# The second layer's first product by Strassen's seven products, with its steps put in order by a list scheduler

## The chip, the cores and the metric

The kernel runs on one core of one Trainium2 chip. The metric is the device time of one execution in microseconds (us), the median of several runs. Engines: PE (TensorE: matmuls; PEld, its weight loads), DVE (VectorE), ACT (ScalarE), POOL (GpSimd), SP (the queue that issues the DMAs).

## What is computed

Windowed attention over 4 batches of 576 tokens gives x, 2304 tokens of 512 values. Two feed-forward layers follow, each with weights `w_in` (512x2048) and `w_out` (2048x512), which arrive as float64:

```
layer 1:  h = x @ w_in;  Q = 1 + |b0|*|h| + |b1|*h*h;  P = a0 + a1*h + a2*h^2 + a3*h^3
          x = (P / (Q + 1e-6)) @ w_out
layer 2:  h = x @ w_in;  g = h if h > 0 else exp(h) - 1
          out = g @ w_out
```

## The kernel before

**Tiling.** The 2304 tokens are cut into 6 blocks of 384 (`TB`), the 2048 hidden values into 16 rows of 128 (`KF`). One row of one block is a chunk: 96 chunks per layer. x lies transposed in `xT` (4 slices of 128 x 2304), and layer 1 writes its result back into it.

**Precision.** Every operand of a product is split into a high and a low fp32r part, and a product runs as three passes (`PASS`: high*high, low*high, high*low). `gemm1` (line 243) makes one chunk of h with 4 slices x 3 passes = 12 matmuls of 128x384. Layer 1's second product (`gemm2_T`, line 696) takes 12 such matmuls per chunk, layer 2's (`gemm2`, line 734) 9 matmuls of 128x512.

**Weights.** A float64 weight tile is joined to float32 and then split: `conv_scale` (ACT), `conv_shift`, `conv_or`, `conv_sign` (three DVE operations on 128x512, lines 145, 152, 159), `conv_hi` (ACT) and `conv_lo` (POOL, line 173). `conv_step` works on three tiles at a time, one at each stage. Layer 1's 32 tiles are converted during attention, the last of them in block 0 of layer 1; layer 2's 32 tiles are loaded and converted from block 5 of layer 1 on, in the slots that layer 1's weights leave (`renew`).

**Order.** All instructions are issued in the order in which the program is written, and each engine works through its own queue in that order. The loop of `experts` (line 764) takes one chunk a turn: `gemm1` of chunk s, then the second product of chunk s-3 (`SK = 3`), then the elementwise work of chunk s. In layer 1 that is `rational` (line 264): on DVE the rest of chunk s-1 and the start of chunk s are interleaved, six operations, and the last one of a chunk, `glo` (line 307), is on POOL. In layer 2 it is `elu` and `elu_split`: two activations on ACT and three operations on DVE. `split_x` makes the fp32r parts of a new block of x.

Of the kernel before, what the change touches and what calls it, by code (L numbers as in the profile page):

```python
# [44 lines left out]
def kernel(  # L45
# [45 lines left out]
    order = [(w, f) for f in range(2 * KF) for w in ("wi", "wo")]  # L91
    order[2 * KF:] = sorted(order[2 * KF:], key=lambda key: 2 * key[1] + 3 * (key[0] == "wo"))
    SLOT = {key: key for key in order[:2 * KF]}


    LATE = order[2 * KF - 8:2 * KF]
    to_load, to_conv = order[:2 * KF], order[:2 * KF]


    ends = {(w, f): f + 3 * (w == "wo") for w, f in order[:2 * KF]}  # L100
    for_x = [("wi", f) for f in range(8)]
    slots = [key for key in sorted(ends, key=ends.get) if key not in for_x] + for_x
    SLOT.update(zip(order[2 * KF:], slots))

# [159 lines left out]
    def rational(c, old=True):  # L264
# [41 lines left out]
        if old:  # L306
            nc.gpsimd.tensor_tensor(out=lo, in0=ee0, in1=rr0, op=ALU.mult)  # L307


# [367 lines left out]
    def experts():  # L677
        es = ctx.enter_context(ExitStack())
        tmp.append(es.enter_context(tc.tile_pool(name="tmp", bufs=1)))
        psum = es.enter_context(tc.tile_pool(name="ps_moe", bufs=1, space=PSUM))  # L680


        def at_rows(c):
            tags = (("h2", "oo"), ("rr0", "rr1"), ("ee0", "ee1"), ("ghi3", "glo3"))[c]
            return [row(t, F32R) for t in tags]

        def at_pieces(j, c):
            t = place(for_x[4 * j + c], [P, 2, TB], F32R, "xs")
            return t[:, 0], t[:, 1]

        def renew(slot):
            key = next(key for key in order[2 * KF:] if SLOT[key] == slot)
            load_w(key)
            to_conv.append(key)
# [20 lines left out]
        def elu(c):  # L715
            h = h_t.pop(c)
            e = row(f"qq{c % 2}")
            nc.scalar.activation(out=e, in_=h, func=AF.Exp)  # L718
# [6 lines left out]
            return e

        def elu_split(c, e):
            hi = row(f"ghi{c % 3}", F32R)
            lo = row(f"glo{c % 3}", F32R)
            nc.scalar.activation(out=hi, in_=e, func=AF.Copy)  # L730
            nc.vector.tensor_tensor(out=lo, in0=e, in1=hi.bitcast(F32), op=ALU.subtract)  # L731
            g_t[c] = (hi, lo)

        def gemm2(c, j, f):
            gt = g_t.pop(c)
            conv_until(to_conv, ("wo", KF + f))
            if f == 0:
                for t in range(NTT):
                    acc_t[j, t] = bank((j % 2) * NTT + t, [P, DM], "acc")
            for t in range(NTT):  # L740
# [6 lines left out]
                if f == KF - 1:
                    o = cv.tile([P, DM], F32, tag="cvt", name="osb")
                    nc.scalar.activation(out=o, in_=acc_t[j, t], func=AF.Copy)
                    r0 = j * TB + t * P  # L750
                    nc.sync.dma_start(out=out[r0:r0 + P, :], in_=o)


        chunks = [(j, f) for f in range(KF) for j in range(2)]
        chunks += [(j, f) for j in range(2, NB) for f in range(KF)]

        SK = 3
        LAST = NCH - KF
        own = {}

        def split_part(parts, j, c, where):
            split_row(parts.setdefault(j, {"hi": [], "lo": []}), j, c, where, nc.vector)
# [87 lines left out]
```

## Time and profile before

| | us |
|---|---|
| median of 3 runs (lowest, highest) | 980.83 (979.93, 981.08) |
| the profiled execution | 979.8 |
| its span, first to last instruction | 978.1 |
| PE busy / DVE / ACT / POOL | 945.8 / 740.6 / 628.3 / 275.9 |

The profile is of one execution. Its busy time of PE counts matmuls whose ends are modelled and that overlap; how fast PE works is read from the distance between the starts of its matmuls. On DVE and ACT, too, the next instruction starts before the record of the one before ends, so what an instruction costs in a full queue is the distance from start to start.

### The profile page before, as it was taken

How to read it: one execution, taken by the hardware profiler on the slowest of the kernel's cores; microseconds unless marked ns; L12 is line 12 of the kernel's file. 1: busy time of each engine (PE TensorE's matmuls, PEld its weight loads, DVE VectorE, ACT ScalarE, POOL GpSimd, SP SyncE). 2: the span in 40 equal slices, each digit the busy share in tenths (PEclk: the TensorE clock that was granted, in tenths of full speed). 3: DMA queues.
4: the chain of work that ended last, by engine and by line, in shares of the span. 5: the costliest groups of instructions: out<-in, count | busy, mean ns of one | idle time of the engine just before them, and what ended most of it. 6: DMA issues, size and time to landing. Idle time of an engine off the chain costs nothing.

```text
span 978.1 us, 16050 instructions
## 1 busy us (share of the span) xinstructions
PE 945.8 (97%) x5638; PEld 865.2 (88%) x5638; DVE 740.6 (76%) x1553; ACT 628.3 (64%) x1368; POOL 275.9 (28%) x315
## 2 busy tenths in 40 slices
PE   7999998989999999999999998999999999999998
PEld 4767667989999999999999986999999999999997
DVE  5999989999998898889889999899543343343332
ACT  5999999779788788788888754555342332322322
POOL 5777764332322222223224342233100000000000
PEclk9999999999999999999999998999999999999999
DMA  6798751000000000000016712200010000000000
GB/s 169 208 248 235 207 160 51 1 1 1 1 1 1 1 1 1 1 1 1 1 44 201 224 50 87 87 1 1 6 60 1 33 1 1 33 1 1 34 1 32
DMA packets 82065, 53.47 MB, mean 55 GB/s; under 512 B 59200, under 2 KB 75584, under 8 KB 81984
## 3 DMA queue, kind: packets, MB, share of 16 engines
q1 hardware_dynamic: 81984, 52.45, 18.2%
q8 instruction: 44, 0.72, 0.3%
q14 instruction: 37, 0.30, 0.1%
HBM read 47.71 MB, written 4.72 MB: 54 GB/s over the span
## 4 chain that ended last, share of the span: by engine, by line
PE 73%; DVE 14%; ACT 9%; issue 3%; DMA 0%; POOL 0%; DVEq 0%; SPq 0%; POOLq 0%; ACTq 0%
PE h L249 35%; PE acc L742 19%; PE acc L705 17%; ACT pT L426 2%; DVE cvt L152 2%; ACT pr_wo L500 2%; ACT pr_wi L500 2%; DVE ghi L287 1%; DVE qq L289 1%; DVE qq L297 1%; DVE ee L305 1%; DVE raw_wo L145 1%; DVE oo L301 1%; ACT cvt L141 1%; DVE cvt L159 1%
## 5 line engine op out<-in xcount | busy, mean ns | idle before, releaser
L249 PE MATMUL h<-xs,w_wi 128*128 128x384 f32 x1260 | 237.4, 335 | 1.8 <-DVE xs L225 0.9
L249 PEld LDWEIGHTS h<-xs,w_wi 128*128 128x128 f32 x1260 | 219.8, 188 | 4.2 <-DVE xs L225 1.5
L705 PE MATMUL acc<-ghi,w_wo 128*128 128x384 f32 x768 | 194.9, 334 | 0.0
L307 POOL TENSOR_TENSOR glo<-ee,rr 128x384 fp32r<-128x384 f32 x96 | 115.7, 1206 | 280.3 <-DVE ee L303 234.6
L742 PE MATMUL acc<-w_wi,ghi 128*128 128x512 f32 x468 | 146.8, 395 | 0.0
L705 PEld LDWEIGHTS acc<-ghi,w_wo 128*128 128x128 f32 x768 | 138.6, 188 | 0.0
L705 PE MATMUL acc<-glo,w_wo 128*128 128x384 f32 x384 | 129.0, 336 | 7.4 <-POOL glo L307 7.4
L718 ACT ACTIVATE qq<-h 128x384 f32<-128x384 f32 x96 | 47.0, 490 | 137.9 <-PE h L249 137.9
L719 DVE TENSOR_SCALAR qq<-qq 128x384 f32<-128x384 f32 x96 | 37.7, 393 | 118.0 <-ACT qq L718 117.2
L730 ACT ACTIVATE ghi<-qq 128x384 fp32r<-128x384 f32 x96 | 50.3, 524 | 97.7 <-PE acc L742 79.8
L287 DVE TENSOR_TENSOR ghi<-ee,rr 128x384 fp32r<-128x384 f32 x96 | 98.5, 1026 | 9.8
L742 PEld LDWEIGHTS acc<-w_wi,ghi 128*128 128x128 f32 x468 | 87.6, 190 | 14.7
L731 DVE TENSOR_TENSOR glo<-qq,ghi 128x384 fp32r<-128x384 f32 x96 | 53.4, 556 | 56.2 <-ACT ghi L730 56.2
L742 PE MATMUL acc<-w_wi,glo 128*128 128x512 f32 x234 | 93.3, 399 | 0.0
L249 PE MATMUL h<-xs,w_wo 128*128 128x384 f32 x408 | 78.2, 338 | 4.6 <-DVE xs L225 3.6
L705 PEld LDWEIGHTS acc<-glo,w_wo 128*128 128x128 f32 x384 | 72.1, 188 | 9.4 <-POOL glo L307 9.3
L249 PEld LDWEIGHTS h<-xs,w_wo 128*128 128x128 f32 x408 | 72.5, 188 | 8.8 <-DVE xs L225 4.2
L289 DVE SCALAR_TENSOR_TENSOR qq<-h,b_abs,qq 128x384 f32<-128x384 f32 x96 | 63.3, 660 | 21.0 <-ACT qq L275 21.0
L293 ACT ACTIVATE rr<-qq,c_q 128x384 f32<-128x384 f32 x96 | 58.9, 614 | 25.5 <-DVE qq L289 24.7
L279 ACT ACTIVATE ee<-h,a_sb 128x384 f32<-128x384 f32 x96 | 67.7, 705 | 4.1 <-POOL glo L307 1.9
L276 ACT ACTIVATE oo<-h,a_sb 128x384 f32<-128x384 f32 x96 | 67.9, 707 | 0.0
L274 ACT ACTIVATE h<-h 128x384 f32<-128x384 f32 x96 | 46.4, 483 | 32.1 <-PE h L249 32.1
(146 smaller groups left out, 1789.8 us busy)
## 6 DMA issues: line engine op xcount, KB each, us to landing
raw_wi<-in_moe_w_in_dram SPq DMA_DIRECT2D x19, 512.0 KB, 4.3
raw_wo<-in_moe_w_out_dram SPq DMA_DIRECT2D x19, 512.0 KB, 4.8
raw_wo<-in_moe_w_in_dram SPq DMA_DIRECT2D x13, 512.0 KB, 4.6
raw_wi<-in_moe_w_out_dram SPq DMA_DIRECT2D x13, 512.0 KB, 4.6
out_dram<-osb SPq DMA_DIRECT2D x18, 256.0 KB, 2.0
v<-in_v_dram SPq DMA_DIRECT2D x32, 128.0 KB, 2.8
q_wi<-in_q_dram SPq DMA_DIRECT2D x16, 128.0 KB, 4.7
k_wi<-in_k_dram SPq DMA_DIRECT2D x16, 128.0 KB, 3.9
```

What stands on the lines that cost most here:

```text
L249: nc.tensor.matmul(h, lhsT=WT["wi", f][:, SEL[wp], kk * P:(kk + 1) * P], rhs=x[xp][kk], start=(kk == 0 and n == 0), stop=(kk == KD - 1 and ...
L276: nc.scalar.activation(out=oo, in_=h2, func=AF.Identity, scale=a_sb[:, 3:4], bias=a_sb[:, 1:2])
L279: nc.scalar.activation(out=ee, in_=h2, func=AF.Identity, scale=a_sb[:, 2:3], bias=a_sb[:, 0:1])
L287: nc.vector.tensor_tensor(out=hi, in0=ee0, in1=rr0, op=ALU.mult)
L289: nc.vector.scalar_tensor_tensor(out=qq, in0=h2, scalar=b_abs[:, 1:2], in1=qq, op0=ALU.mult, op1=ALU.add)
L293: nc.scalar.activation(out=rr, in_=qq, func=AF.Ln, bias=c_q)
L307: nc.gpsimd.tensor_tensor(out=lo, in0=ee0, in1=rr0, op=ALU.mult)
L705: nc.tensor.matmul(acc_t[d], lhsT=WT["wo", f][:, SEL[wp], d * P:(d + 1) * P], rhs=gt[SEL[xp]], start=(f == 0 and n == 0), stop=(f == KF - ...
L718: nc.scalar.activation(out=e, in_=h, func=AF.Exp)
L730: nc.scalar.activation(out=hi, in_=e, func=AF.Copy)
L731: nc.vector.tensor_tensor(out=lo, in0=e, in1=hi.bitcast(F32), op=ALU.subtract)
L742: nc.tensor.matmul(acc_t[j, t], lhsT=gt[SEL[xp]][:, t * P:(t + 1) * P], rhs=WT["wo", KF + f][:, SEL[wp], :], start=(f == 0 and n == 0), st ...
```

## The change

**Strassen.** Layer 2's `gemm1` goes. Two neighbouring weight rows (a pair, p = 0 to 7) and two neighbouring blocks (J = 0 to 2) make a step q = 8J + p, 24 in all, and the four chunks of a step come from seven products (`product`) of half the depth, 2 slices x 3 passes = 6 matmuls of 128x384 each: 42 where four calls of `gemm1` had 48. The operands are a11, a12, a22 and four sums s1 to s4 of quarters of the weights (`sum_w`, four POOL operations of 128x256 per step), and b11, b21, b22 and four differences t1 to t4 of quarters of x (`sum_x`, eight operations of 128x384 per J; on DVE for J = 0, on POOL for J = 1 and 2). The seven results are put together by one copy on ACT (`copy_of`) and seven additions on DVE (`added`, line 943). All of them pass through two PSUM banks in turn.

**The elementwise work of layer 2** is now exp, minus one (ACT), one DVE operation (`rest`, line 958), the high part (ACT) and the low part (DVE, `lo`, line 847). Per step DVE also makes the low parts of six weight operands (five 128x512, one 128x256), and per J those of 14 operands of x.

**Weights of layer 2.** Twenty of the 32 tiles (`early_ones`) are loaded in halves during blocks 0 to 4 of layer 1, joined there (`join_scale` on ACT, `join_words` with three DVE operations of 128x256) and stored as float32 in DRAM; `load_wi` and `load_wo` read them back in every J. 40 half tiles are joined, ten in each of blocks 1 to 4. The other twelve `w_out` tiles are joined in steps 0 to 7 (one tile in steps 0 to 3, two in 4 to 7) by `join_wo`, three DVE operations of 128x512.

**Layer 1.** `glo` moves from POOL to DVE. In block 5 `prepare` makes the operands of step 0 that can be made by then.

**Order of layer 2.** `second(q)` describes each piece of work as a step with an engine, a cost in ns and what it needs. `in_order` simulates the engines with these costs: PE's steps keep the order in which they are written, the other engines take, of the steps that are ready within 60 ns of the earliest, the one due first. The program is then issued in the order of the starts that it found.

```diff
@@ rational
+        if beside:
+            beside()
...
-            nc.gpsimd.tensor_tensor(out=lo, in0=ee0, in1=rr0, op=ALU.mult)
+            nc.vector.tensor_tensor(out=lo, in0=ee0, in1=rr0, op=ALU.mult)
@@ experts: layer 1's loop
-        for s in range(2 * NCH + SK):
+        for s in range(NCH):
...
+            if j > 0 and f % 3 and f < KF - 1 and nj < 2 * len(early_ones):
+                rational(s, beside=lambda: join_words(nj))
+                nj += 1
+            else:
+                rational(s)
+            if j > 0 and f % 3 < 2 and f < KF - 2:
+                join_scale(nj)
+                load_half(nj + 1)
...
+            if s >= LAST:
+                prepare(s - LAST)
+        rational(NCH)
+        for q in range(NQ):
+            second(q)
+        for fn in in_order():
+            fn()
+        last_pair()
@@ experts: layer 2
+        def product(q, nm):
+            x, side = LIES[FACTOR[nm]]
+            w = OPS[q, x]
+            out = bank((4 if q == 0 else 6) + next(ny), [P, TB], "m")
+            for k in range(2):
+                c0 = side * HC + k * P
+                for n, (wp, xp) in enumerate(PASS):
+                    nc.tensor.matmul(
+                        out, lhsT=w[:, SEL[wp], c0:c0 + P], rhs=XO[q // NP2, nm, k][:, SEL[xp]],
+                        start=(k == 0 and n == 0), stop=(k == 1 and n == 2),
+                    )
+            return out
...
+        def second(q):
+            p = q % NP2
+            multiply(q, "b11", (q - 1, "h21"))
+            multiply(q, "b21", (q - 1, "h12"))
+            second_product(q, 0)
+            multiply(q, "t2", (q, "m1"))
+            multiply(q, "t3", (q, "h11"))
+            second_product(q, 1)
+            multiply(q, "t1", (q, "u"))
+            second_product(q, 2)
+            multiply(q, "t4", (q, "v"))
+            multiply(q, "b22", (q, "h22"), (q, "u2"))
+            second_product(q, 3)
...
+        def prepare(f):
+            if f == 1:
+                load_wi(0)
+            if 3 <= f < 7:
+                sum_x(0, f - 3, nc.vector)
+            if f == 7:
+                sum_w(0, nc.vector)
+            if 8 <= f < 12:
+                hi_w(0, "ABCD"[f - 8])
+                lo((0, "ABCD"[f - 8]))
+            if 7 <= f < 11:
+                for k in range(2):
+                    hi_op(0, ORDER[f - 7], k)
+                for k in range(2):
+                    lo((0, ORDER[f - 7], k))
```

`second_product(q, n)` is the second product (9 matmuls of 128x512) of one chunk of step q-1; `last_pair` makes those of the last step.

**Where instructions move.** DVE in the middle of layer 1, one chunk. Before:

```order
L287 TENSOR_TENSOR ghi_5826<-ee_5776,rr_5785 128x384
L289 SCALAR_TENSOR_TENSOR qq_5819<-h_5818,b_abs,qq_5819 128x384
L297 SCALAR_TENSOR_TENSOR qq_5774<-qq_5774,ghi_5826 128x384
L301 TENSOR_TENSOR oo<-oo,h 128x384
L303 TENSOR_TENSOR ee_5776<-ee_5776,qq_5774 128x384
L305 TENSOR_TENSOR ee_5821<-ee_5821,oo 128x384
```

And now, a chunk that joins half a weight tile:

```order
L286 TENSOR_TENSOR ghi_4331<-ee_4278,rr_4287 128x384
L288 SCALAR_TENSOR_TENSOR qq_4324<-h_4323,b_abs,qq_4324 128x384
L764 TENSOR_SCALAR half_4199<-half_4199 128x256
L768 SCALAR_TENSOR_TENSOR whole_3175<-whole_3175,half_4199 128x256
L771 SCALAR_TENSOR_TENSOR whole_3175<-half_4199,whole_3175 128x256
L298 SCALAR_TENSOR_TENSOR qq_4276<-qq_4276,ghi_4331 128x384
L302 TENSOR_TENSOR oo<-oo,h 128x384
L304 TENSOR_TENSOR ee_4278<-ee_4278,qq_4276 128x384
L306 TENSOR_TENSOR ee_4326<-ee_4326,oo 128x384
L308 TENSOR_TENSOR glo_4332<-ee_4278,rr_4287 128x384
```

The low part (`glo`) has come from POOL to the end of the chunk's row, and three operations on half a weight tile stand ahead of the rest of the older chunk.

DVE in layer 2, from the first addition of a step with two raw `w_out` tiles (`qq`, `ee`: the sums of products `m`; `op`: weight operands; `pair`: the joined `w_out`):

```order
L943 TENSOR_TENSOR qq_8128<-qq_8107,m 128x384
L847 TENSOR_TENSOR rr_8113<-oo,rr_8112 128x384
L847 TENSOR_TENSOR op_wo_8124<-s_8069,op_wo_8124 128x512
L847 TENSOR_TENSOR op_wi_8126<-s_8070,op_wi_8126 128x512
L943 TENSOR_TENSOR ee_8155<-qq_8107,m 128x384
L958 SCALAR_TENSOR_TENSOR h_8142<-h_8142,qq_8128 128x384
L943 TENSOR_TENSOR ee_8167<-ee_8155,m 128x384
L138 TENSOR_SCALAR raw_wo_8089<-raw_wo_8089 128x512
L145 SCALAR_TENSOR_TENSOR pair<-pair,raw_wo_8089 128x512
L152 SCALAR_TENSOR_TENSOR pair<-raw_wo_8089,pair 128x512
L847 TENSOR_TENSOR glo_8170<-h_8142,ghi_8169 128x384
L847 TENSOR_TENSOR op_wi_8130<-pair,op_wi_8130 128x512
```

The additions that empty the PSUM banks (line 943) stand between the splits of weights and the joining of a tile for later steps.

PE in layer 2, from the start of a step; each x3 is half of a product, each x2 with the row behind it a third of a second product:

```order
L887 MATMUL m<-xo_wo_6762,op_wi_7546 128x384 x3
L887 MATMUL m<-xo_wi_6764,op_wi_7546 128x384 x3
L887 MATMUL m<-xo_wo_6816,op_wi_7546 128x384 x3
L887 MATMUL m<-xo_wi_6818,op_wi_7546 128x384 x3
L903 MATMUL acc<-op_wo_7601,ghi_7811 128x512 x2
L903 MATMUL acc<-op_wo_7601,glo_7812 128x512
L903 MATMUL acc<-op_wo_7601,ghi_7811 128x512 x2
L903 MATMUL acc<-op_wo_7601,glo_7812 128x512
L903 MATMUL acc<-op_wo_7601,ghi_7811 128x512 x2
L903 MATMUL acc<-op_wo_7601,glo_7812 128x512
L887 MATMUL m<-xo_wo_6870,op_wo_7672 128x384 x3
L887 MATMUL m<-xo_wi_6872,op_wo_7672 128x384 x3
```

Where one chunk's product of 12 matmuls and one second product took turns, two products of 6 matmuls now stand before most of the second products.

## Rows read from the trace of the kernel before

**Rows 1.** Busy time by stretch: us, PE, PEld, DVE, ACT, POOL, PEclk, DMA share, GB/s.
```profile
160.00:200.00 40.00, 36.85 (x210) 35.89 (x209) 39.01 (x61) 31.21 (x59) 14.31 (x12) 1.00 0.00 1
440.00:480.00 40.00, 40.00 (x232) 40.00 (x232) 36.48 (x62) 32.23 (x61) 11.74 (x10) 1.00 0.00 1
600.00:640.00 40.00, 35.47 (x162) 31.32 (x163) 35.58 (x59) 19.45 (x39) 10.43 (x8) 0.91 0.15 53
760.00:800.00 40.00, 40.00 (x202) 36.20 (x201) 15.71 (x33) 12.88 (x26) 0.00 (x0) 1.00 0.05 21
```

**Rows 2.** Chain that ended last: start us, length us, engine, tile, line, instructions.
```profile
607.91 3.84 PE acc L742 x9
611.75 2.67 PE h L249 x12
...
622.80 2.08 PE acc L742 x9
...
964.00 2.10 PE h L249 x12
966.10 8.22 PE acc L742 x36
```

**Rows 3.** Waits of PE over the whole span: us in total, times, longest.
```profile
PE acc L705 <- POOL glo L307: 7.4, 6, 1.5
...
PE h L249 <- DVE xs L225: 4.5, 3, 3.0
...
PE h L249 <- ACT xs L224: 1.6, 3, 0.7
```

**Rows 4.** Busy time by stretch around the longest wait.
```profile
602.00:606.00 4.00, 1.06 (x3) 0.48 (x3) 3.84 (x6) 2.12 (x4) 1.33 (x1) 1.00 0.00 0
606.00:610.00 4.00, 2.77 (x7) 2.31 (x8) 3.06 (x6) 1.99 (x4) 0.90 (x1) 0.50 0.01 2
```

**Rows 5.** DVE in order of time, one chunk of layer 1: start us, length us.
```profile
304.48 1.16 DVE L287 TENSOR_TENSOR ghi<-ee,rr 128x384 fp32r<-128x384 f32 x1
305.56 0.61 DVE L289 SCALAR_TENSOR_TENSOR qq<-h,b_abs,qq 128x384 f32<-128x384 f32 x1
306.09 0.55 DVE L297 SCALAR_TENSOR_TENSOR qq<-qq,ghi 128x384 f32<-128x384 f32 x1
306.56 0.54 DVE L301 TENSOR_TENSOR oo<-oo,h 128x384 f32<-128x384 f32 x1
307.02 0.55 DVE L303 TENSOR_TENSOR ee<-ee,qq 128x384 f32<-128x384 f32 x1
307.49 0.55 DVE L305 TENSOR_TENSOR ee<-ee,oo 128x384 f32<-128x384 f32 x1
308.17 1.16 DVE L287 TENSOR_TENSOR ghi<-ee,rr 128x384 fp32r<-128x384 f32 x1
```

**Rows 6.** POOL in order of time, the same chunk.
```profile
304.05 1.17 POOL L307 TENSOR_TENSOR glo<-ee,rr 128x384 fp32r<-128x384 f32 x1 [4.99 <-DVE ee L303]
```

**Rows 7.** DVE in order of time: one weight tile joined in layer 2.
```profile
641.04 1.27 DVE L145 TENSOR_SCALAR raw_wo<-raw_wo 128x512 int32<-128x512 int32 x1
642.41 0.69 DVE L152 SCALAR_TENSOR_TENSOR cvt<-cvt,raw_wo 128x512 int32<-128x512 int32 x1
643.14 0.69 DVE L159 SCALAR_TENSOR_TENSOR cvt<-raw_wo,cvt 128x512 int32<-128x512 int32 x1
643.75 0.55 DVE L731 TENSOR_TENSOR glo<-qq,ghi 128x384 fp32r<-128x384 f32 x1
```

**Rows 8.** POOL in order of time, beside it.
```profile
640.73 1.29 POOL L173 TENSOR_TENSOR w_wi<-cvt,w_wi 128x512 fp32r<-128x512 f32 x1 [2.88 <-ACT w_wi L169]
```

**Rows 9.** Line 145 during attention: duration in ns, least/median/most.
```profile
L145 DVE TENSOR_SCALAR raw_wo<-raw_wo x14: 406/420/427, 31.5 to 153.8; 128x512 int32<-128x512 int32 x14
```

**Rows 10.** DMA issues on the page: instructions, KB each, median us to landing.
```profile
raw_wo<-in_moe_w_out_dram SPq DMA_DIRECT2D x19, 512.0 KB, 4.8
```

**Rows 11.** Groups by line, 720 to 960 us: busy us, mean ns of one.
```profile
L731 DVE TENSOR_TENSOR glo<-qq,ghi 128x384 fp32r<-128x384 f32 x57 | 31.9, 559 | 48.2 <-ACT ghi L730 48.2
L730 ACT ACTIVATE ghi<-qq 128x384 fp32r<-128x384 f32 x58 | 30.4, 524 | 74.1 <-PE acc L742 67.6 <-DVE qq L722 6.6
```

More of the change, by code (lines that the diff above doesn't have):

```diff
@@ L83 @@
     c_q = const.tile([P, 1], F32, name="c_q")
+    c_m = const.tile([P, 1], F32, name="c_m")
     xT = const.tile([P, KD, NT], F32, name="xT")
@@ L90 @@
     WT = {}
[L91 to L103, printed above, removed]
+    order = [(w, f) for f in range(KF) for w in ("wi", "wo")]
+    SLOT = {key: key for key in order}
+    LATE = order[2 * KF - 8:]
+    to_load, to_conv = order[:], order[:]
     RAW = {}
@@ L262, in early, with rational @@
             yield from gemm1(c, c, x1[0], 4 + c)
-    def rational(c, old=True):
+    def rational(c, old=True, beside=None):
         old = old and c - 1 in q_t
@@ L637, in attention @@
             nc.gpsimd.memset(c_q, EPSC)
+            nc.gpsimd.memset(c_m, -1.0)
             for t in pt:
@@ L677, in experts @@
     def experts():
[L678 to L694, printed above, removed]
+        tmp.append(ctx.enter_context(tc.tile_pool(name="tmp", bufs=1)))
         def gemm2_T(c):
@@ L713, in gemm2_T @@
                     )
[L715 to L718, printed above, removed]
-            nc.vector.tensor_scalar(
-                out=e, in0=e, scalar1=1.0, scalar2=-1.0, op0=ALU.min, op1=ALU.add
+        NP2, NJ, HC = KF // 2, NB // 2, PC // 2
+        NQ = NJ * NP2
+        LAST = NCH - KF
+        wi, wo = [("wi", f) for f in range(KF)], [("wo", f) for f in range(KF)]
+        t_slots = [wi[2], wi[3], wo[0], wi[4]]
@@ L721, in elu @@
             )
             nc.vector.scalar_tensor_tensor(
-                out=e, in0=h, scalar=0.0, in1=e, op0=ALU.max, op1=ALU.add
+                out=wi, in0=high, scalar=-2147483648, in1=wi, op0=ALU.bitwise_and, op1=ALU.bitwise_or
             )
[L725 to L740, printed above, removed]
+            key = early_ones[n // 2]
+            if n % 2 == 0:
+                joined[key] = dram.tile([P, PC], F32, name="joined_%s_%d" % key)
+            nc.sync.dma_start(out=joined[key][:, n % 2 * HC:(n % 2 + 1) * HC], in_=w)
@@ new lines, in at, with raw_ones, load_raw, load_wi @@
+        def at(q, letter, shape, dtype, what):
+            nm = "_".join(map(str, SETS[q % 3][letter]))
+            return wpool.tile(shape, dtype, tag=nm, name=f"{what}_{nm}")
+        def raw_ones(q):
+            return [e for e in range(2) if q < NP2 and ("wo", KF + 2 * q + e) not in early_ones]
+        def load_raw(q, e):
+            key = ("wo", KF + 2 * q + e)
+            SLOT[key] = SETS[q % 3]["EF"[e]]
+            load_w(key)
+        def load_wi(q):
+            two[q] = t = at(q, "C", [P, 2, PC], F32, "two")
+            for e in range(2):
+                nc.sync.dma_start(out=t[:, e], in_=joined["wi", KF + q % NP2 * 2 + e])
@@ new lines, in both, with load_wo, scale_wo, join_wo @@
+        def both(e):
+            if not pair:
+                pair.append(xs.tile([P, 2, PC], F32, tag="x0", name="pair"))
+            return pair[0][:, e]
+        def load_wo(q, e):
+            nc.sync.dma_start(out=both(e), in_=joined["wo", KF + q % NP2 * 2 + e])
+        def scale_wo(q, e):
+            key = ("wo", KF + 2 * q + e)
+            T32[key] = both(e)
+            nc.scalar.activation(out=both(e), in_=words(key)[1].bitcast(F32), func=AF.Copy, scale=2.0 ** -112)
+        def join_wo(q, e):
+            key = ("wo", KF + 2 * q + e)
+            conv_shift(key)
+            conv_or(key)
+            conv_sign(key)
+            del RAW[key]
@@ new lines, in hi_op @@
+        def hi_op(J, nm, k):
+            if nm[0] == "t":
+                src = sums[J, int(nm[1]) - 1][k]
+            else:
+                src = x_row(J, k + 2 * (nm[1] == "2"), nm[2] == "2")
+            s = "_".join(map(str, x_slots[2 * ORDER.index(nm) + k]))
+            XO[J, nm, k] = t = wpool.tile([P, 2, TB], F32R, tag=s, name=f"xo_{s}")
+            nc.scalar.activation(out=t[:, 0], in_=src, func=AF.Copy)
+            low_part[J, nm, k] = (t[:, 1], src, t[:, 0])
+        ny = cycle((0, 1))
@@ L747, in gemm2 @@
[L747 to L755, printed above, removed]
-        SK = 3
[L758 to L762, printed above, removed]
```

361 lines of the change are left out of this document (311 added, 50 removed).

## The prediction

> **What bounds the kernel now.** I read the busy time by stretch first. In the middle of both layers PE works without a gap, 232 and 202 matmuls in 40 us, while DVE is busy 36.48 and 15.71 us [rows 1]. Two stretches fall short: 160 to 200 us, where DVE is busy 39.01 of 40 us and PE starts 210 matmuls, and 600 to 640 us, the turn from layer 1 to layer 2, with 162 matmuls and a granted clock of 0.91 [rows 1]. The chain of what ended last gives PE's rates: 12 matmuls of 128x384 take 2.10 us (0.175 each), 9 of 128x512 take 2.08 us [rows 2], so a chunk costs PE 2.10 + 2.08 = 4.18 us. The waits of PE say what was late: `glo`, from POOL, six times for 7.4 us, and the parts of new blocks of x for 4.5 and 1.6 us [rows 3]. After the longest, 3.0 us, the granted clock is 0.50 (1.2 of 2.4 GHz) in 606 to 610 us, with PE busy 1.06 us in the four before [rows 4]; 9 matmuls then take 3.84 us and 12 take 2.67 [rows 2], 1.76 + 0.57 = 2.3 us more than at full clock.
>
> So PE's work is the bound, and where it isn't, DVE is.
>
> **PE's work.** A step now has 42 matmuls in its first products and four second products: 42 x 0.175 + 4 x 2.08 = 15.67 us. Before, its four chunks took 4 x 4.18 = 16.7 us; the difference is 6 matmuls, 1.05 us. Over 24 steps: **-25.2 us**. The form (128x128 weights, 384 columns) is the old one, so I take its row. [...]
>
> **Waits that go.** (1) `glo` on DVE. One chunk of layer 1 takes a full DVE queue 308.17 - 304.48 = 3.69 us; `ghi` alone stands 1.16 us, where an undisturbed operation of this size has 0.55 and comes 0.47 us after the one before [rows 5]. It is held by POOL's `glo` of 1.17 us [rows 6]. Now seven operations of 0.47 us and the slower L289 (0.06 more) make 3.35 us. Block 0 also joins the last four weight tiles: 0.42 + 0.73 + 0.61 = 1.76 us each, and 0.85 us more where POOL is in the way, 1.27 instead of 0.42 beside POOL's 1.29 [rows 7 to 9]. With a new block of x (4 x 0.47) DVE had 16 x 3.69 + 4 x 2.6 + 1.9 = 71 us for 16 x 4.18 = 67 us of PE, and now has 66. `glo` also no longer queues behind a weight tile on POOL. Of the 7.4 us I take **-5.4** (bounds 0 and -7.4). (2) The turn: layer 2's weights are no longer converted there. Of the 6.1 us of waits for x I take 4.5, and the slow clock's 2.3: **-6.8** (bounds -3 and -8.4).
>
> **Waits that come.** (3) Blocks 1 to 4. A join of half a tile: the first operation between half of 0.42 and 0.42, the others 0.37 and 0.33 (0.55 and 0.69 for 384 and 512 columns make 0.41 for 256, in a full queue 0.08 less), with their dependences 1.1 us. Ten in 16 chunks, and x: 16 x 3.35 + 10 x 1.1 + 1.9 = 66.5 of PE's 66.9 us. DVE is full, but the second product runs three chunks behind, which absorbs a surge: **+2** (0 to 8). The half tiles' loads have two chunks of lead, 8.4 us, and 512 KB landed in 4.8 us [rows 10], so they hide; without that cover DVE stands in the middle of `rational` (a rival below). ACT, 32.23 of 40 us [rows 1], gets ten activations of under 0.5 us per 67 us, and has room. (4) Block 5: `prepare` adds 8 + 8 operations of 0.47 us, four of 0.45 and four splits (3 x 0.61 + 0.33), 11.5 us. That fits into the block (53.6 + 11.5 = 65 of 67 us), but chunks 7 to 10 alone hold 20.5 us against 16.7: **+2** (0 to 5).
>
> (5) Steps 0 to 8. DVE has per step 7 additions, 4 `rest` and 4 `lo` (15 x 0.47), and the weights' splits (5 x 0.61 + 0.33): 10.4 us. Nine steps: 93.6, less 2.2 done in block 5; twelve joins of `w_out` x 1.76 = 21.1; 20 splits of x, 9.4. POOL's sums hold DVE as `glo` did: 1.29 us for 512 columns [rows 8], so 0.65 for 256, 2.6 us a step. Of POOL's time DVE lost 0.61 of 1.17 and 0.85 of 1.29 [rows 5 to 9], half to two thirds: 1.6 us a step, 14.4 in nine, and 4.8 for the eight sums of x (1.0 each). The sum is 141 us, and PE's nine steps are 9 x 15.67 = 141. Yet the products pass through two PSUM banks, and a product starts only when DVE or ACT has emptied its bank; PE has some 3.1 us of other work (one product, one second product) between, and a DVE queue that is full comes late now and then: a joined tile (1.76) in front of two additions (0.94) with one hold by POOL (0.65) makes 3.35 us. I price 0.8 us a step: **+7** (0 to 22, the end at 2.5 us a step). (6) Steps 9 to 23: 10.4 + 0.8 (x) + 1.9 (POOL) = 13.1 of 15.67 us; ACT, with some 19 activations of 0.52 us [rows 11], 10 us. 0.2 us a step: **+3** (0 to 10). (7) The end: the last low part hangs on a chain of six operations (about 0.55 each) behind t4, over which PE has b22, one second product and a third of another, 3.8 us: **+1** (0 to 2). The copies and stores behind the last matmul at 974.3 us [rows 2] stay.
>
> What goes or comes elsewhere costs nothing that I can see: the stores and loads of joined weights (2 MB a step at most) lie about two steps ahead of their use, and ACT has 5 us a step to spare.
>
> **Sum**, against the profiled execution's 979.8: -25.2 - 5.4 - 6.8 + 2 + 2 + 7 + 3 + 1 = -22.4, so 957.4. The median of the runs shown is 1.0 us above that execution: **958 us**.
>
> **Rivals.**
> *The covers hold.* DVE loses less to POOL than assumed, since a hold that falls into one of its pauses costs nothing; its queue falls full only in places, and the new waits come to 3 us instead of 15. Then 946; with none, 943, and with all of the old waits gone 940. For it: before, DVE at 36 of 40 us let PE run without a gap [rows 1]. Against: at 39 of 40 it did not. Chance 0.27.
>
> *DVE sets layer 2's pace.* Each POOL operation holds DVE for its whole length: 2.6 us a step and 8 for the sums of x, which makes DVE's nine steps 153 us, 12 more than PE's, and in the other steps about 1 us is lost at each pass through the banks, 24 in all where I count 10: new waits of 28 to 36 us, 970 to 979. For it: `ghi` lost 0.61 us in every chunk of layer 1 [rows 5]. Against: that is half of POOL's 1.17, not all [rows 6]. The Trainium skill (SBUF — State Buffer, SBUF: two separate sides) says that the path that DVE and GpSimd share is an exclusive lock, kept for the whole instruction, and that it concerns DVE operations with two SBUF inputs. By that rule alone the nine steps are these 153 us; the trace shows the hold, but only part of it as a loss. Chance 0.13.
>
> *Slower, by joins that wait.* The first operation of a join stands in DVE's queue between the two chunks of `rational` and needs its half tile from DRAM, the second needs the activation before it, and that needs the store of two halves ago. If the loads or stores come late, everything behind on DVE waits, `glo` with it, and PE. Forty joins must then lose 23 us more than I count to reach 980.8, 0.6 us each; at 1.5 us each the time is 958 + 60 = 1018. Against: 4.8 us to land 512 KB [rows 10] within 8.4 us of lead, for half the bytes, on queues that moved nothing in 440 to 480 us [rows 1]. Chance 0.04.
>
> *The saving is not there*: the products' matmuls wait for weights or banks at each change, as many as were saved (six of 0.175 us, 1.05 us a step), and the new waits of DVE eat what the old ones gave: 980 or so. Chance 0.02.
>
> **How the numbers follow.** My forecast (947 to 969) has 0.54, the rest as above. 0.2%, about 2 us, is what a measurement can tell from no change. Faster: 0.54 + 0.27 + 0.13 = 0.94, less 0.01 for a third case that goes beyond its top: 0.93. Same: 0.02. Slower: 0.04 and that 0.01, 0.05. The range reaches from 941 (the covers hold, nearly all old waits gone) into the lower part of the third case, 972, which leaves out some 0.2.
>
> **What would show it.** In the changed profile: PE's products at 6 matmuls in 1.05 us and steps of 15.7 us from step 9 on; granted clock 1.00 through the turn; no wait of PE for `glo` from POOL, and few for DVE in layer 1; DVE at 39 of 40 us in blocks 1 to 4 and in steps 0 to 8, with PE's waits there for additions of line 943, the longest between t1 and b22; DVE operations with two SBUF inputs of 0.8 to 1.2 us beside POOL's sums. I am wrong if steps 9 to 23 take over 16.2 us, if `join_words` waits for DMA, or if PE in steps 0 to 8 shows no waits at all.

## The result and the profile after

The change takes **967.51 us** (median of 4 runs, 965.85 to 968.59); the kernel before, run beside it, took 980.38 us (979.63 to 981.08). The ratio is 0.9866, 95% interval 0.9849 to 0.9883: 12.9 us faster, where the forecast was 22.8 (958 against 980.83). The profiled execution took 965.85 us, its span 963.8.

Busy time on the page of the change:

```profile
PE 927.3 (96%) x5494; PEld 842.7 (87%) x5494; DVE 864.8 (90%) x1949; ACT 750.6 (78%) x1628; POOL 232.7 (24%) x296
```

DVE is busy 124 us longer than before, POOL 43 us less. By stretch (columns as in [rows 1]):

```profile
160.00:200.00 40.00, 40.00 (x231) 39.77 (x231) 39.46 (x75) 33.52 (x65) 5.96 (x4) 1.00 0.00 1
440.00:480.00 40.00, 40.00 (x233) 40.00 (x232) 39.48 (x89) 34.51 (x68) 0.00 (x0) 1.00 0.20 60
560.00:600.00 40.00, 33.15 (x150) 29.77 (x149) 38.36 (x66) 28.85 (x58) 13.85 (x14) 0.87 0.31 95
600.00:640.00 40.00, 36.44 (x179) 31.89 (x178) 38.42 (x69) 26.95 (x53) 12.94 (x12) 1.00 0.33 117
680.00:720.00 40.00, 37.14 (x183) 32.73 (x182) 35.65 (x60) 29.87 (x63) 17.82 (x16) 1.00 0.31 102
760.00:800.00 40.00, 40.00 (x201) 36.07 (x200) 31.23 (x56) 26.76 (x53) 11.28 (x12) 1.00 0.23 67
```

Block 0 has its 231 matmuls now (210 before). The turn has not got better, only moved: 150 matmuls and a granted clock of 0.87 in 560 to 600 us, where before 600 to 640 had 162 and 0.91. Waits of PE over the whole span, answering to [rows 3]:

```profile
PE m L887 <- DVE ee L943: 6.8, 5, 2.4
PE m L887 <- ACT qq L937: 3.7, 1, 3.7
PE h L248 <- DVE xs L224: 3.4, 5, 0.8
PE m L887 <- DVE qq L943: 3.3, 4, 1.6
PE acc L691 <- DVE glo L308: 1.8, 4, 0.8
```

The waits for `xs` and `glo` stand at layer 1's products; the others, 13.8 us, stand at L887, where a product of layer 2 needs a bank. The chain in the undisturbed part of layer 2, answering to [rows 2] (start, length, what):

```profile
720.36 2.10 PE m L887 x12
722.47 2.08 PE acc L903 x9
724.55 1.06 PE m L887 x6
725.62 2.08 PE acc L903 x9
```

I call step n the time from the start of product t1 of step n-1 to that of its own. Steps 9 to 23 take 15.70 to 15.87 us, 15.73 on average.

Where the time went (PE's work at its undisturbed pace: 0.175 us a matmul of 384 columns, 2.08 us for 9 of 512):

| us | before | after |
|---|---|---|
| first regular chunk of layer 1 (chunk 4 of block 0) to the first product of layer 2 | 389.7 | 390.5 |
| from there to the end of the last matmul | 420.3 | 405.1 |
| of it PE's work at that pace | 407.5 | 382.3 |
| of it lost | 12.8 | 22.8 |

So the saved matmuls came in full and layer 2 lost 10 us more than before. Of the 22.8, 10.1 lie at the turn (first product to t1 of step 0: 18.48 us, for work of 8.4), some 11 in steps 1 to 8 (134.9 us, where e10 below takes 124.0), 0.4 in steps 9 to 23; the rest is small gaps.

**The turn**, in order of time. POOL:

```profile
555.29 1.05 POOL L830 TENSOR_TENSOR s<-two_wo,s 128x256 f32<-128x256 f32 x1
556.30 7.70 POOL L866 TENSOR_TENSOR xT<-xT 128x384 f32<-128x384 f32 x6
```

DVE beside it:

```profile
556.68 1.37 DVE L308 TENSOR_TENSOR glo<-ee,rr 128x384 fp32r<-128x384 f32 x1
557.97 1.36 DVE L286 TENSOR_TENSOR ghi<-ee,rr 128x384 fp32r<-128x384 f32 x1
559.25 1.36 DVE L288 SCALAR_TENSOR_TENSOR qq<-h,b_abs,qq 128x384 f32<-128x384 f32 x1
560.53 1.35 DVE L298 SCALAR_TENSOR_TENSOR qq<-qq,ghi 128x384 f32<-128x384 f32 x1
561.80 0.54 DVE L302 TENSOR_TENSOR oo<-oo,h 128x384 f32<-128x384 f32 x1
562.27 0.88 DVE L304 TENSOR_TENSOR ee<-ee,qq 128x384 f32<-128x384 f32 x1
```

ACT and PE:

```profile
560.64 0.61 ACT L292 ACTIVATE rr<-qq,c_q 128x384 f32<-128x384 f32 x1 [1.85 <-DVE qq L288]
563.24 0.49 ACT L937 ACTIVATE qq<-m 128x384 f32<-128x384 f32 x1 [1.43 <-DVE ee L304]
```

```profile
563.79 1.33 PE L887 MATMUL m<-xo_wo,op_wi 128*128 128x384 f32 x3 [3.68 <-ACT qq L937]
567.72 1.33 PE L887 MATMUL m<-xo_wo,op_wi 128*128 128x384 f32 x3 [1.65 <-DVE qq L943]
```

The list put the eight differences of x for J = 1 (L866) into POOL's queue right behind the first sums of weights (L830), and POOL ran six of them at the turn, though step 8, over 100 us later, is the first to use them. Six of them stand 7.70 / 6 = 1.28 us apart, and so do DVE's operations on two SBUF tiles, 1.28 instead of 0.47; L302, which reads h from PSUM, keeps 0.47. So `rational`'s last operations are late, ACT waits for them in the middle of its queue, and the copy of b11 (L937), which empties the bank for t2, stands behind and waits for L304. After PE's gap of 3.9 us the granted clock is 0.50 (1.2 of 2.4 GHz):

```profile
560.00:564.00 4.00, 0.32 (x2) 0.22 (x2) 4.00 (x5) 1.90 (x4) 4.00 (x4) 0.95 0.41 131
564.00:568.00 4.00, 2.35 (x7) 1.84 (x8) 3.83 (x8) 3.02 (x8) 0.00 (x1) 0.50 0.01 2
568.00:572.00 4.00, 4.00 (x13) 4.00 (x14) 4.00 (x9) 3.17 (x7) 1.85 (x2) 0.50 0.00 0
```

The waits of 0.3, 3.7 and 1.65 us and some 4 us that the matmuls took longer at that clock are the turn's 10.1 us.

### The profile page after: what moved, and what is told of

The parts are those of the page before. It is cut to its first block, busy times and chain, and to the rows that moved or that the text cites. A ratio compares the mean times of both kernels' runs of the same rounds, so it can differ in the third digit from the quotient of the medians.

```text
span 963.8 us, 16615 instructions
## 1 busy us (share of the span) xinstructions
PE 927.3 (96%) x5494; PEld 842.7 (87%) x5494; DVE 864.8 (90%) x1949; ACT 750.6 (78%) x1628; POOL 232.7 (24%) x296
## 4 chain that ended last, share of the span: by engine, by line
PE 56%; DVE 20%; ACT 13%; issue 7%; SPq 2%; DMA 1%; DVEq 0%; ACTq 0%
PE acc L691 15%; PE h L248 14%; PE acc L903 14%; PE m L887 12%; ACT pT L427 2%; ACT pr_wo L501 2%; ACT pr_wi L501 2%; DVE qq L288 2%; DVE ghi L286 2%; DVE qq L298 2%; DVE op_wo L847 1%; DVE op_wi L847 1%; DVE oo L302 1%; SPq L334 1%; DVE ee L943 1%
## 5 line engine op out<-in xcount | busy, mean ns | idle before, releaser
L830 POOL TENSOR_TENSOR s<-two_wo 128x256 f32<-128x256 f32 x32 | 33.3, 1041 | 503.5 <-DMA two_wo<-joined_wi 379.6
L887 PE MATMUL m<-xo_wo,op_wi 128*128 128x384 f32 x336 | 79.1, 343 | 12.1 <-DVE ee L943 4.8
L903 PE MATMUL acc<-op_wo,ghi 128*128 128x512 f32 x288 | 89.6, 392 | 0.0
L887 PEld LDWEIGHTS m<-xo_wo,op_wi 128*128 128x128 f32 x336 | 60.9, 191 | 20.2 <-DVE ee L943 6.4
L887 PE MATMUL m<-xo_wi,op_wi 128*128 128x384 f32 x336 | 78.2, 341 | 0.0
L274 ACT ACTIVATE qq<-h,b_abs 128x384 f32<-128x384 f32 x96 | 55.4, 577 | 23.8 <-DVE ee L304 23.8
L887 PEld LDWEIGHTS m<-xo_wi,op_wi 128*128 128x128 f32 x336 | 61.4, 190 | 0.0
L903 PEld LDWEIGHTS acc<-op_wo,ghi 128*128 128x128 f32 x288 | 53.5, 188 | 8.9
L903 PE MATMUL acc<-op_wo,glo 128*128 128x512 f32 x144 | 57.0, 396 | 0.0
L943 DVE TENSOR_TENSOR ee<-ee,m 128x384 f32<-128x384 f32 x96 | 52.4, 545 | 4.2 <-PE m L887 4.2
L306 DVE TENSOR_TENSOR ee<-ee,oo 128x384 f32<-128x384 f32 x96 | 54.5, 568 | 0.2
```

What stands on the lines that cost most here:

```text
L274: nc.scalar.activation(out=qq, in_=h, func=AF.Abs, scale=b_abs[:, 0:1])
L306: nc.vector.tensor_tensor(out=ee, in0=ee, in1=oo, op=ALU.add)
L887: nc.tensor.matmul(out, lhsT=w[:, SEL[wp], c0:c0 + P], rhs=XO[q // NP2, nm, k][:, SEL[xp]], start=(k == 0 and n == 0), stop=(k == 1 and n ...
L903: nc.tensor.matmul(acc_t[T, t], lhsT=gt[SEL[xp]][:, t * P:(t + 1) * P], rhs=w[:, SEL[wp]], start=(first and n == 0), stop=(last and n == 2),)
L943: nc.vector.tensor_tensor(out=t, in0=R[q, x], in1=M[q, m], op=ALU.add)
```

## The experiments

The experiments look for what makes VectorE late. Theory A: GpSimd's sums take time from VectorE's operations on two SBUF inputs. Rival B: VectorE's own queue is overfull there (joins, preparation), and GpSimd stands beside it by chance. Rival C: the sums hurt by coming late to their users. All kernels start from the change. The stretches: T, from the first second product of layer 1 to t1 of step 0; U, steps 1 to 8; V, steps 9 to 23. What lies ahead of T (attention, the same in all but for how the first DMAs fall) was 161.1 to 164.2 us, so differences of 2 us in the time alone mean little. e1 to e4 and e12 ran on one chip, e5 to e11 on another; each ratio is to the kernel before on the same chip.

| kernel | us | ratio to before, 95% | T | U | V |
|---|---|---|---|---|---|
| the change | 967.51 | 0.9849 to 0.9883 | 411.0 | 134.9 | 236.0 |
| e1 sums of x (J = 1) later | 966.74 | 0.9853 to 0.9886 | 406.0 | 139.4 | 236.0 |
| e2 the same, J = 2 | 965.75 | 0.9841 to 0.9870 | 411.7 | 132.7 | 237.6 |
| e3 all sums on DVE | 948.14 | 0.9661 to 0.9690 | 402.4 | 125.6 | 235.6 |
| e4 late joins in three pieces | 965.50 | 0.9835 to 0.9864 | 411.5 | 132.5 | 237.6 |
| e5 sums of x on DVE | 960.30 | 0.9787 to 0.9817 | 407.0 | 133.9 | 236.6 |
| e6 sums of weights on DVE | 957.87 | 0.9762 to 0.9794 | 407.0 | 130.8 | 235.6 |
| e7 `glo` back on POOL | 1000.65 | 1.0195 to 1.0231 | 442.3 | 140.5 | 236.1 |
| e8 no early joins | 960.86 | 0.9799 to 0.9828 | 405.8 | 135.1 | 236.1 |
| e9 no late joins | 958.40 | 0.9765 to 0.9797 | 409.1 | 128.4 | 237.8 |
| e10 = e3 + e4 | 945.84 | 0.9641 to 0.9669 | 402.4 | 124.0 | 235.6 |
| e11 = e3, early joins moved | 947.30 | 0.9662 to 0.9689 | 402.4 | 125.6 | 235.6 |
| e12 = e3 + e4 + e11 | 946.21 | 0.9641 to 0.9670 | 402.3 | 124.0 | 235.6 |

**e1.** The eight sums of x for J = 1 may start only behind `h11`, the first of the four chunks that a step puts together, of steps 1 to 4, two in each.

```diff
-                step(("sum", J, n), "POOL", 2300, lambda n=n: sum_x(J, n), *used, *[("sum", J, i) for i in range(n)])
+                step(("sum", J, n), "POOL", 2300, lambda n=n: sum_x(J, n), *used, *[("sum", J, i) for i in range(n)],
+                     *([(1 + n, "h11")] if J == 1 else []))
```

> Theory A (GpSimd's sums of x for the second pair of blocks, which the list puts at the turn from layer 1 to layer 2 though nobody needs them for 120 us, hold VectorE's two-input operations there): in the trace of the change ten VectorE operations of rational's last chunk grow by 0.1 to 0.82 us each between 552.6 and 564.3, some 6 us, of which some 4.5 stand beside L866. With these sums put behind the weights' sums of steps 2 to 5, VectorE's operations of 556 to 564 should fall to 0.54 to 1.1 us, TensorE's wait of 3.68 us at L887 should fall under 1 us, its clock should hardly fall to half after it, and the time should come to 958 to 963 us (against 967.5), less what the same sums now cost beside steps 2 to 5 (up to 1 us each). Rival B (VectorE's queue is simply overfull at the turn, by the joins and the preparation of block 5, and GpSimd stands beside it by chance): the wait at L887 stays over 3 us and the time at 966 to 969.

Measured: 966.74 us, the number that rival B gave. The trace says otherwise: at the turn DVE is back at 0.47 us from start to start, PE's wait at L887 is 0.7 instead of 3.7, and the granted clock in 564 to 568 us is 0.74 instead of 0.50. DVE's instructions stand there in the same order as in the change, up to 583.7 us in step 1. DVE and PE at the turn, and POOL in step 1:

```profile
558.52 0.54 DVE L308 TENSOR_TENSOR glo<-ee,rr 128x384 fp32r<-128x384 f32 x1
558.99 0.55 DVE L286 TENSOR_TENSOR ghi<-ee,rr 128x384 fp32r<-128x384 f32 x1
```

```profile
562.10 0.79 PE L887 MATMUL m<-xo_wo,op_wi 128*128 128x384 f32 x3 [0.67 <-ACT qq L937]
565.24 0.79 PE L887 MATMUL m<-xo_wo,op_wi 128*128 128x384 f32 x3 [1.82 <-DVE qq L943]
```

```profile
578.99 2.75 POOL L866 TENSOR_TENSOR xT<-xT 128x384 f32<-128x384 f32 x2
```

T got 5.1 us shorter and U 4.5 us longer: steps 1 to 4 take 14.64, 19.04, 19.64 and 18.60 us, in the change 14.07, 17.62, 19.58 and 16.19. No product needs these sums in steps 1 to 4, so they cost time there by standing beside DVE; a part may come from the list, which also changed the order of DVE in 35 places from 583.7 us on. That supports theory A. The price, 1.1 us a pair, is as high as the gain at the turn, and with it theory A's time cannot be told from rival B's; only the stretches tell them apart.

**e2.** The same line for J = 2, behind `(NP2 + 1 + n, "h11")`.

> The same for the third pair of blocks alone (its eight sums, 10.26 us at 700.9, spread over four steps). Theory A: step 8, which takes 19.03 us against 15.70 of an undisturbed step, falls to 15.7 to 17, and the time to 964.5 to 966. Rival B (step 8 is late by the 14 splits of x that its list of operands changes, not by GpSimd): step 8 stays at 18.5 to 19.5 us and the time at 967 to 968.

Step 8 fell from 19.03 to 16.84, as theory A has it, and step 10 rose from 15.86 to 17.49: moved again, with 2.2 us gained in U and 1.5 lost in V. 965.75 us is within what the start can shift. This is the cleanest of the comparisons: after attention DVE, ACT and PE work through the same instructions in the same order as in the change, and only POOL's order differs. Of the three pairs that moved, the one in step 10 costs 1.6 us, those in steps 11 and 12 nothing (15.71 and 15.73 us): here a sum on POOL costs PE time only where DVE has none to spare.

**e3.** All sums of layer 2 on DVE.

```diff
-                step((w, "sum"), "POOL", 2900, lambda: sum_w(w), (w, "load"), ...
+                step((w, "sum"), "DVE", 1500, lambda: sum_w(w, nc.vector), (w, "load"), ...
...
-                step(("sum", J, n), "POOL", 2300, lambda n=n: sum_x(J, n), *used, ...
+                step(("sum", J, n), "DVE", 940, lambda n=n: sum_x(J, n, nc.vector), *used, ...
```

> All sums of layer 2 (of x for the second and third pair, of the weights for 23 steps) on VectorE instead of GpSimd. VectorE takes some 0.47 us for 128x384 and, by the half of a 128x512 one, some 0.3 us for 128x256: 16 x 0.47 + 92 x 0.33 = 38 us more on an engine that is busy 90% of the span, 1.3 us in each of steps 1 to 23. Theory A (a sum on GpSimd holds VectorE for as long as VectorE would need itself, or longer): the turn and step 8 get better by some 6 to 9 us, the regular steps stay at 15.7, and the time is 956 to 963 us. Rival B (GpSimd's work is really beside VectorE's): VectorE becomes the engine that sets layer 2's pace, regular steps grow to 16 to 17 us, and the time is 975 to 995 us.

948.14 us, 19 us faster than the change and 8 better than theory A's best; rival B's 975 is far off. The page of e3:

```profile
PE 921.4 (97%) x5494; PEld 841.2 (89%) x5494; DVE 867.5 (92%) x2057; ACT 749.0 (79%) x1628; POOL 120.0 (13%) x188
```

DVE has 108 instructions more and is busy 2.7 us longer: what it now does itself it had lost before. Four sums of weights and the next operation on DVE:

```profile
591.69 0.42 DVE L830 TENSOR_TENSOR s<-two_wi 128x256 f32<-128x256 f32 x1
592.15 0.42 DVE L830 TENSOR_TENSOR s<-s,two_wi 128x256 f32<-128x256 f32 x1
592.49 0.42 DVE L830 TENSOR_TENSOR s<-two_wi 128x256 f32<-128x256 f32 x1
592.82 0.42 DVE L830 TENSOR_TENSOR s<-two_wi,s 128x256 f32<-128x256 f32 x1
593.16 0.55 DVE L943 TENSOR_TENSOR qq<-qq,m 128x384 f32<-128x384 f32 x1
```

1.47 us for the four. In the change the same four held three operations of DVE (592.61 to 595.66, 3.05 us instead of 1.54), a loss of 1.5 us (2.0 beside the set at the turn of e1):

```profile
592.61 0.97 DVE L847 TENSOR_TENSOR glo<-h,ghi 128x384 fp32r<-128x384 f32 x1
593.50 1.22 DVE L847 TENSOR_TENSOR op_wo<-pair,op_wo 128x512 fp32r<-128x512 f32 x1
594.65 1.09 DVE L958 SCALAR_TENSOR_TENSOR oo<-oo,qq 128x384 f32<-128x384 f32 x1
595.66 0.68 DVE L847 TENSOR_TENSOR op_wo<-two_wi,op_wo 128x512 fp32r<-128x512 f32 x1
```

So a set of weights' sums costs DVE as much on POOL as on itself, or more; a sum of x costs it 0.81 us on POOL and 0.47 on DVE. That alone does not make 19 us. What else e3 changes: the list now counts the sums as DVE's time and puts them by their due time (L866 for J = 1 from 664.6 us on), and a set of four is ready after 1.5 us instead of some 4. The runs do not divide the gain among these.

**e4.** A late join in three pieces on the list.

```diff
-                    step((w, "words", x), "DVE", 1600, lambda e=e: join_wo(w, e), (w, "scale", x))
+                    step((w, "shift", x), "DVE", 420, lambda key=key: conv_shift(key), (w, "scale", x))
+                    step((w, "or", x), "DVE", 620, lambda key=key: conv_or(key), (w, "shift", x))
+                    step((w, "words", x), "DVE", 610, lambda key=key: join_wo(key), (w, "or", x))
```

> The join of a word pair of w_out in layer 2's first pass, 1.6 us that stand as one piece in VectorE's queue, is put on the list as three pieces (shift, or, sign), so that additions on which TensorE waits can come between. In steps 2 to 4 of the change the waits of 0.7, 0.7, 2.35 and 1.1 us of TensorE stand behind such joins. If the piece's length is the cause: steps 2 to 4 (17.62, 19.58, 16.19 us) lose 2 to 4 us together and the time is 963.5 to 966. If the amount of VectorE's work in these steps is the cause: no change, 967 to 968 us.

965.50 us. Steps 2 to 4 lost 3.2 us (16.67, 17.32, 16.20), as expected if the piece's length counts, and steps 7 to 9 got 3.0 us longer (16.62, 19.60, 17.34). With the sums on POOL this order only moved the loss; in e10, with the sums on DVE, the same edit takes 1.6 us off steps 1 to 8 and adds nothing elsewhere.

**e5 and e6.** Each half of e3 alone.

> Only the 16 sums of x go to VectorE; the weights' sums stay on GpSimd. Theory A, as the first runs left it (a sum on GpSimd takes from VectorE's two-input work wherever it stands, so moving it in time only moves the loss, as with the sums put later, whose turn got 3.6 us better and whose steps 1 to 4 got 4.5 us worse): the 16 sums are 3.7 us of the turn and some 3 us of step 8, less 16 x 0.47 us of VectorE's own, half of it in steps with room: 961 to 965 us, the turn's wait at L887 under 1 us, step 8 at 16 to 17 us, steps 2 to 4 still over 16 us. Rival C (the weights' sums alone are what hurts, through their lateness for operands C and D): no change, 966 to 968.

> Only the weights' sums (92 of 128x256) go to VectorE; the sums of x stay on GpSimd. Theory A: steps 2 to 6 (17.62, 19.58, 16.19, 16.37, 16.36 us) fall to 15.7 to 16.2, the turn's wait of 3.7 us and step 8's 3.3 us mostly stay: 953 to 960 us. Rival C: everything that was gained with both on VectorE (19.4 us) is gained here, 947 to 950. Rival B (too much work of VectorE's own): slower than 967.

e5: 960.30 us, a little below its range. The turn's long wait is 0.7 us and step 8 takes 16.36, but steps 2 and 3 stay at 17.58 and 19.58, and step 5 takes 18.85: rival C is refuted as the only cause. e6: 957.87 us, within theory A's range; steps 2 to 4 take 15.92, 15.71 and 15.71, and step 8 still 20.18. The turn's wait, which was to stay, is gone (first product to t1: 9.55 us), because the loss moved once more: without the weights' sums, which waited on POOL for their load until 550.67 us in the change, five of the sums of x ran at 529 to 538 us, in block 5, and two chunks there took 6.26 and 7.88 instead of 4.16 us. POOL and DVE in block 5 of e6:

```profile
529.08 3.91 POOL L866 TENSOR_TENSOR xT<-xT 128x384 f32<-128x384 f32 x3
529.46 1.37 DVE L288 SCALAR_TENSOR_TENSOR qq<-h,b_abs,qq 128x384 f32<-128x384 f32 x1
```

Alone the two halves bring 7.2 and 9.6 us, together 19.4. So both sorts of sum hurt, each where it stands.

**e7.** The part of the change in layer 1 undone: `nc.gpsimd.tensor_tensor` for `glo` in `rational`.

> The change with glo of layer 1 back on GpSimd (the undone part). By VectorE's own rows: a chunk takes 3.69 us with glo on GpSimd (before) and 3.34 us with it on VectorE (after), a block of 16 chunks then 59.0 or 53.4 us, to which 8 or so joins of halves of 1.13 us and four splits of 0.47 us come, 70 or 64.4 us against TensorE's 66.7. Theory A: VectorE sets the pace of the blocks with joins, 3 us more for each, and the turn gets later: 978 to 988 us in all. Rival (GpSimd's glo stands beside VectorE's work for free): VectorE is relieved, the waits of 3.4 us at the turns of the blocks go, 963 to 966 us.

1000.65 us, over the range: the direction is theory A's, its size is 33 us instead of 11 to 21. Stretches of e7 in blocks with joins:

```profile
290.00:360.00 70.00, 66.52 (x359) 64.46 (x359) 65.00 (x122) 56.31 (x108) 17.54 (x15) 0.95 0.17 52
490.00:550.00 60.00, 57.05 (x308) 55.66 (x307) 54.93 (x99) 46.85 (x89) 16.62 (x13) 0.94 0.09 27
```

DVE in a chunk with a join:

```profile
307.28 1.16 DVE L286 TENSOR_TENSOR ghi<-ee,rr 128x384 fp32r<-128x384 f32 x1
310.15 0.62 DVE L288 SCALAR_TENSOR_TENSOR qq<-h,b_abs,qq 128x384 f32<-128x384 f32 x1 [1.71 <-ACT qq L274]
```

`ghi` stands 1.16 us as in [rows 5]. My price was DVE's full queue, 70 us a block, but turns of blocks lie 73.4 to 74.9 us apart: DVE is not even full (65.00 of 70), it also waits for ACT, ACT for PE and PE for `glo`, and the granted clock is 0.94 and 0.95. Which of these adds how much stays open.

**e8.** In `join_words` the three DVE operations go.

> Left out: the three VectorE operations that join a half word tile in layer 1 (the loads, the scaling and the stores stay, so the second layer's weights are wrong). What they cost in the change: by the forecast 2 us in blocks 1 to 4. If they are covered by VectorE's room: the waits for parts of x at the turns of the blocks (3.4 us) go and little else, 962 to 966 us; and the waits of layer 2, which come after them, stay. If VectorE comes late to the turn because of them (rival B): the wait of 3.7 us at the turn goes as well, 955 to 961.

960.86 us, below the first range and within the one for rival B; but layer 1 is 3.9 us shorter and the turn's wait stays (its line, 887 in the change, is 877 here):

```profile
PE m L877 <- ACT qq L927: 3.7, 1, 3.7
PE m L877 <- DVE qq L933: 3.4, 4, 1.8
...
PE h L248 <- DVE xs L224: 0.6, 1, 0.6
```

The joins cost the waits for `xs` at the turns of the blocks, a chunk of 5.1 to 5.2 instead of 4.16 us at each of four turns. They do not make the long wait at the turn, which refutes rival B's joins there; the other half of rival B, the preparation in block 5, stands unchanged in e1, where that wait falls to 0.7 us.

**e9.** In `join_wo` the three operations go; order as in the change.

> Left out: the three VectorE operations that join a word tile of w_out in steps 0 to 7 of layer 2 (12 tiles of 1.6 us; so the second layer's weights are wrong); all sums stay on GpSimd, and the order stands as in the change. Theory A with the sum of the runs so far (VectorE's time in steps 1 to 8 is overdrawn by its own work, the joins among it, and by what the sums take, so that either of the two off it brings a step back to TensorE's 15.70): steps 2 to 6, which took 17.62, 19.58, 16.19, 16.37 and 16.36 us, come to 15.7 to 16.3, step 8 stays near 19, the turn stays; 960 to 963 us. Rival (the sums hurt by coming late to the operands C and D, joins or not): steps 2 to 6 stay over 16.3, 965 to 968.

958.40 us, a little below the range. Steps 2 to 6 take 15.96, 16.21, 15.71, 15.71 and 15.70, step 8 18.35 and step 9 17.32. So the joins or the weights' sums, either one off, bring steps 2 to 6 back: DVE's time there is overdrawn by both, and neither is the cause alone. Rival C, by which these steps were to stay over 16.3 us while the sums are on POOL, is refuted there. The turn, which was to stay, takes 15.86 instead of 18.48 us.

**e10 to e12.** e10 is e3 with e4's three pieces. e11 is e3 with the early joins away from the turns of the blocks; e12 has all.

```diff
+        JOINS = (1, 2, 3, 4, 5, 7, 8, 9, 10, 11)
...
-            if j > 0 and f % 3 and f < KF - 1 and nj < 2 * len(early_ones):
+            if j > 0 and f in JOINS and nj < 2 * len(early_ones):
...
-            if j > 0 and f % 3 < 2 and f < KF - 2:
+            if j > 0 and f + 1 in JOINS:
```

> All sums of layer 2 on VectorE and the late joins in three pieces. With the sums on VectorE, layer 2 has only some 2 us left that its products do not fill (steps 0 to 1 15.91, step 4 16.50 us against 15.70): 946.5 to 948.5 us. If the list's other order brings a new wait, as it did in steps 6 to 9 with the pieces alone: 949 to 951.

> All sums on VectorE, and the ten joins of halves of each of the blocks 1 to 4 of layer 1 done in chunks 1 to 5 and 7 to 11 instead of the chunks 1, 2, 4, 5 to 13, 14. Without any early joins TensorE's waits for parts of x at the turns of the blocks were gone (3.5 to 0.6 us). If these waits come from the joins just ahead of the turn: they go here too, 944 to 946.5 us. If they come from the joins' sum (VectorE is 98% busy in these blocks): 947.5 to 949, or new waits for glo in the chunks of the joins, 949 to 952.

> The three together: all sums of layer 2 on VectorE, the late joins in three pieces, the early joins off the turns of the blocks. Layer 2 was 385.2 us of its products and their waits with the first two (ideal 382.3), layer 1 loses 3.5 us at the turns of its blocks without the third. If the gains add: 942 to 944.5 us. If the joins' new places in layer 1 make VectorE late to layer 2: 945 to 947.

e10: 945.84 us, ratio 0.9655; steps 2 to 23 all take 15.70 or 15.71 us. In the profiles it takes 1.6 us less than e3 in steps 1 to 8; the rest of the difference is the start. After layer 1, PE has one wait above 0.3 us:

```profile
PE m L884 <- DVE qq L940: 1.2, 1, 1.2
```

e11: 947.30, no gain over e3 that can be told. The waits for `xs` went (3.5 to 0.6 us), but five chunks of each of these blocks now take 4.2 to 4.5 us instead of 4.16, about 1 us a block again: in these two orders it is the joins' amount on a full DVE that costs, not their place. e12: 946.21, the same as e10: the gains did not add, since e11 had none to add (T is 402.3 as in e3). e10 and e12, which the times do not tell apart, are the best: 34 us faster than the kernel before and some 22 us faster than the change.

## Why the prediction was right and wrong

The sign, the bound and the mechanism of the gain were right; the gain was 14.4 us between the same points of the two profiles (810.0 to 795.6) instead of 22.4.

**PE's work, -25.2: right.** 12 matmuls in 2.10 us and 6 in 1.06, steps of 15.70 us where 15.67 was worked out.

**(1), (3), (4), layer 1: near, +0.7 us where -1.4 was forecast.** Over 4.16 us a chunk, block 0 lost 7.0 us before and 2.5 now (-4.5; two of the six old waits for `glo` lay in the turn and belong to (2)); blocks 1 to 4 lose 4.0, not 2, and e8 shows that it is the joins; block 5 loses 1.2, not 2. `join_words` never waited for DMA. e7 shows that `glo` on DVE is what pays for the joins: with `glo` back on POOL the kernel takes 33 us more.

**(2), the turn, -6.8: the step that failed.** I took the old losses there away and put nothing in their place. The old losses did go (12 of the 12.8 us lay in the first twelve chunks of layer 2), but new ones of 10.1 us came: a gain of 2, not of 6.8, and the granted clock, which was to stay at 1.00, fell to 0.50. The eight sums of x for J = 1, for which (5) has 4.8 us of DVE's time (0.6 each), I spread over steps 0 to 8, since step 8 is their user. The list puts a step on an idle engine as soon as it is ready, whoever needs it, and counts nothing for what it does to another engine; so the sums fell upon the turn (in e6 upon block 5), where DVE had no time to spare. Of the 10.1 us the turn loses, e1 takes away 5.5 (first product to t1: 12.93 instead of 18.48) and e3 8.5.

**(5), +7: right in place and kind, too small.** Steps 1 to 8 lose some 11 us, at line 943 as foretold. The longest wait, in step 3, stands between t4 and b22, as foretold too: a join and two held splits stand ahead of the addition at 611.44 us that frees the bank.

```profile
612.05 0.79 PE L887 MATMUL m<-xo_wo,op_wi 128*128 128x384 f32 x3 [2.35 <-DVE ee L943]
```

The price for POOL's weights' sums (1.6 us a step) is about the 1.5 us measured above; for x it was 0.6 a sum, and 0.81 was measured. What was too low is what a full queue costs: with DVE's 141 us of work on PE's 141, I allowed 0.8 us a step.

**(6), +3: too high; (7), +1: nothing.** Steps 9 to 23 lose 0.4 us together, and from t1 of the last step to the end of the last matmul there are 15.7 us, for work of 15.6. So a part of what (2) and (5) left out was made up by (6) and (7), which was luck.

**The rivals.** Had the covers held, 943 to 946 was the time: the change was 22 us above that, and e10 reaches it. That DVE sets layer 2's pace (970 to 979) had the right engine and the right cause but too large a price. By the Trainium skill (SBUF — State Buffer, SBUF: two separate sides), the path that DVE and GpSimd share is an exclusive lock, which a DVE instruction with two SBUF inputs or a GpSimd instruction holds for its whole length. The trace agrees: POOL's six sums and DVE's operations stand 1.28 us apart, one of each in turn, and the operation that reads PSUM is not held. What it adds is the price: in each 1.28 us DVE still gets an operation of its own, 0.47 us, so that it loses 0.81 to a sum, not 1.28.

## What to carry to other kernels

Where VectorE is full, an elementwise operation on two SBUF tiles was not taken off it here by giving it to GpSimd: count what it takes from VectorE there, and first try it on VectorE itself. A list scheduler that knows engines but not what they share puts early work on the idle engine at the worst place; give such work a due time, or count it on the engine that pays. And an experiment that only moves a cost can leave the time unchanged and still show the cost: read where it went, stage by stage.

## What was not expected of the hardware

One GpSimd difference of 128x384 takes 0.81 us from a full VectorE, which makes it itself in 0.47; four of 128x256 took 1.5 to 2.0 us and take VectorE 1.47. On VectorE, 108 operations more left its busy time at 867.5 against 864.8 us. GpSimd loses too: its 128x256 sums take 0.73 us alone and mostly 0.9 to 1.3 beside VectorE's.
